# A sparse-attention and gMLP kernel: fewer row-halved score tiles, v of a pair in one load, gMLP sums in two parts, and another order

## The chip, the cores and the metric

The kernel runs on one core of a Trainium2 chip. Time is device microseconds (us) of one execution; the kernel before took 218.75 us, the median of three runs (218.19 to 218.76). The engines of the core are TensorE (PE: matmuls; PEld: its weight loads), VectorE (DVE), ScalarE (ACT), GpSimd (POOL) and SyncE (SP, which here only issues DMA). Each runs its own instructions in order and waits for others by semaphores. Matmuls write PSUM; this kernel has four banks `PSG` for general use and two double banks `PSC` for scores.

## The reference, cut

Two stages follow each other. First attention over chosen chunks of keys, for 4 batches of 8 heads, 768 positions, 64 numbers a head; then a gMLP block on the result, with 512 model and 1024 hidden columns.

```python
def _attn_ref(q, k, v):                                   # (4, 8, 768, 64) each
    k_min, k_max = ...                                    # of each chunk of 32 keys
    ub = np.sum(np.maximum(q[..., None, :] * k_min, q[..., None, :] * k_max), axis=-1)
    ub = np.where(causal, ub, -1e9)
    top_chunks = np.argsort(ub, axis=-1)[..., -6:]        # six chunks for each query
    scores = scale * np.matmul(q, k.transpose(0, 1, 3, 2))
    scores = np.where(sel & (pos[:, None] >= pos[None, :]), scores, -1e9)
    attn = softmax(scores)                                # written out in the original
    return np.matmul(attn, v)

def _moe_ref(x, w_in, g_ln, w_sg, b_sg, w_out):           # x: (4, 768, 512)
    h = gelu_tanh(x @ w_in)                               # written out in the original
    u, v = h[..., :512], h[..., 512:]
    v_n = layer_norm(v) * g_ln
    v_s = np.einsum('ts,bsd->btd', w_sg, v_n) + b_sg[None, :, None]
    return x + (u * v_s) @ w_out
```

## The kernel before

The program is a list of named operations, each with an engine, what it reads and writes, and the PSUM tile that it takes. A long string `ORDER` names all of them in the order in which they are to be issued; each engine takes those of its own from it, one after another. A word such as `ka5.1@dve` puts an operation on another engine than its usual one, and `kt1.1:0` gives it PSUM slot 0. Semaphore waits follow from the reads and writes. `FILL` puts matmuls on zeros ahead of some operations of TensorE, where it waits.

The names: for a pair p of heads (16 pairs, four to a batch) `lk lq lv` load k, q and v, `kt qt` transpose k and q on TensorE, `kn kx` take the minimum and maximum of each chunk, `ke ka kb` and `qe` take the transposed k and q out of PSUM, `qr` is the positive part of q, `qc qa qb` copy q to bf16, `ub` to `uq` select the chunks of one group of pairs, `d` copies masks into place, `vc` casts v. For a head h, `s` are its scores, `e` the exponentials, `af` the causal cut on the diagonal blocks, `pv pd` the product with v, `xr xs` the division, `xt xe` the transpose for the gMLP. For a batch, `hv gv bs ba re rp rm rn vh` make the normalised half of the hidden columns, `hu gu` the other half, `pt vs gm` the mixing over positions with `w_sg` and the product of the halves, `ou oa os` the output. `wsg wt we` load and transpose `w_sg`.

Scores have two forms. The pairs below `NHALF` are row-halved: both heads of the pair lie in one tile of 128 rows, 64 each, and their matmuls use half of the array's rows each; the mask of the chosen chunks is added by matmuls of its own, with 32 rows of contraction (lines of the kernel 719 and 726):

```python
                def sc(e, t=t, m=m, segs=segs):
                    ...
                    for (o, n, kb, q0) in segs:
                        ...
                                e.matmul(t.ap()[:, 512 * i + o + a - q0:512 * i + o + n],
                                         IND[32 * cg:32 * cg + 32, 128 * kb:128 * kb + 128],
                                         dt_[32 * cg:32 * cg + 32, a - d0:z - d0], start=fresh[i], stop=False,
                                         skip_group_check=True, tile_position=(32 * cg, 0))
                    for (o, n, kb, q0) in segs:
                        for i in range(2):
                            r = e.matmul(t.ap()[:, 512 * i + o:512 * i + o + n],
                                         KP[p][64 * i:64 * i + 64, 128 * kb:128 * kb + 128],
                                         QP[p][64 * i:64 * i + 64, q0:q0 + n], start=fresh[i], stop=True,
                                         skip_group_check=True, tile_position=(64 * i, 0))
```

All other pairs are whole: each head has a tile of its own in which k (or q) and the mask lie on different rows, so one matmul of 96 or 128 rows makes the masked score (line 766). The masks have to be copied into those rows, by small DMAs `d`:

```python
            kt_, qt_, rows = (KA[w], QA[w], slice(0, 96)) if i == 0 else (KB[w], QB[w], slice(0, 128))
            ...
                def sc(e, t=t, mms=mms):
                    for (o, n, kb, q0) in mms:
                        r = e.matmul(t.ap()[:, o:o + n], kt_[rows, 128 * kb:128 * kb + 128],
                                     qt_[rows, q0:q0 + n], start=True, stop=True, skip_group_check=True)
```

A whole pair has its k taken out of PSUM in four instructions (`ka`, `kb`), a row-halved pair in two (`ke`); its q is copied to bf16 in two instructions (`qa`, `qb`) instead of one (`qc`).

The parts of the gMLP that the change touches, each an accumulation in one PSUM bank:

```python
                def hv(e, t=t, qt=qt):
                    for dk in range(NDK):                      # 4
                        r = e.matmul(t.ap()[:, 0:F], xT[s][:, dk, 128 * qt:128 * qt + 128], winb[:, dk, F:DFF],
                                     start=(dk == 0), stop=(dk == NDK - 1))
                ...
                    def pt(e, t=t, fb=fb, tg=tg):
                        for sb in range(NT):                   # 6
                            r = e.matmul(t.ap()[:, 0:TG], vhat[s][:, sb, 128 * fb:128 * fb + 128],
                                         wsgT[:, sb, TG * tg:TG * tg + TG], start=(sb == 0), stop=(sb == NT - 1))
                ...
                    def ou(e, t=t, qt=qt):
                        for fb in range(NF):                   # 4
                            r = e.matmul(t.ap()[:, 0:DM], gT[s][:, fb, 128 * qt:128 * qt + 128], woutb[:, fb, :],
                                         start=(fb == 0), stop=(fb == NF - 1))
```

`oa` adds x to the output tile on VectorE into one of three buffers `osb`, and `os` stores it. Loads are limited to six in flight (`WINDOW`); k, q and v have three buffers each (`NQS`), in pieces of 256 bytes:

```python
            for i in range(2):
                o, pat, off = dst[s][:, :, i, :], [[DH, 128], [128 * DH, NT], [1, DH]], (2 * p + i) * S * DH
                P.op(f"l{nm[0]}{p}.{i}", "sp", lambda e, o=o, pat=pat, off=off: e.dma_start(
                    o, bass.AP(src.tensor, off, pat)),
                    writes=[(nm, s, i)], dma=f"{nm}{s}_{i}", bulk=True, cost=(560, 905), prio=prio + i)
```

Of the kernel before, what the change touches and what calls it, by code (L numbers as in the profile page):

```python
# [9 lines left out]
BF16 = mybir.dt.bfloat16  # L10
# [8 lines left out]
nh lk1.0 zB2 warm0 lk1.1 J0 lk0.0 zA0 idF lk0.1 J vx13 W02 W03 W01 W00 vx10 lq0.1 lq0.0 kt1.1:0 kt1.0:1 kn1.1 lq1.0  # L19
kn1.0 kx1.1 lq2.1 kt0.1:2 kx1.0 kt0.0:3 kn0.1 lq1.1 ke1.0 kw1@pool zA1 kn0.0 ke1.1 lq2.0 qt0.1:1 kx0.0 qt0.0:0 qe0.1  # L20
Jn kx0.1 lk2.1 qe0.0 qr0.1 kw0@pool qr0.0@act qc0 lk2.0 ke0.0 vx11 IND ub0:10 ke0.1 iB1 lq3.1 qt1.1:3 ut0.1 qt1.0:2
ut0.0 qe1.1 lq3.0 uc0.10 uc0.00 qe1.0 uc0.11 uc0.01 uc0.12 uc0.02 um0.1 qr1.0@act qc1 lk3.0 qt2.1:0 qr1.1@act um0.0
qt2.0:1 qe2.1 ud0.1 ub1:23 lk4.1 qe2.0 ud0.0 uq0.1 iA0 qr2@act uq0.0 lk3.1 kt2.1:0 ut1.0 s0.4:0 ut1.1 s0.2:1 uc1.00
e0.4 kn2.1 lk4.0 uc1.01 uc1.10 s0.3:0 e0.2 uc1.02 kx2.1 lv0.0 uc1.11 kt2.0:1 um1.0 qt3.1:2 e0.3 lv0.1 uc1.12 kn2.0
s0.0:1 ud1.0 ke2.1 lq4.1 um1.1 af1.1 s0.5:0 e0.0 idB kx2.0 lk5.0 kt3.0:3 ud1.1 e0.5 kt3.1:0 ke2.0@dve af0.0 s0.6:1
lq4.0 uq1.1 kn3.1 kt4.1:1 qe3.1 s0.1:0 e0.6 uq1.0 lk5.1 vc0 kx3.1 qt3.0:2 e0.1 s1.0:1 kn4.1 af1.0 qe3.0 lq5.0 kn3.0
ke3.1 af0.2 s1.1:0 e1.0 af1.2 kx4.1 lq6.0 pv1:2 af0.1 kx3.0 pd1 qc2 pv0:0 ka4.1 lq6.1 xr1 ke3.0@dve pd0 s1.5:1 kb4.1
af2.0 xr0 xs1 lk6.1 e1.1 qt4.0:3 kw3@pool af3.0 xs0 qt4.1:1 e1.5 kt4.0:2 lq5.1 qr3 xt0.0:0 kn4.0 kw2@pool s1.3:0 qe4.0
af2.2 lv1.1 xe0.0 qe4.1 iB3 kt5.0:3 e1.3 kx4.0 lv1.0 ub2:10 kn5.0 kw4@pool qc3 ka4.0 lk6.0 kx5.0 kb4.0 s1.2:1 ut2.0
af3.2 ka5.0 lq7.1 ut2.1 qt6.0:2 e1.2 uc2.10 uc2.00 um2.1 lv3.1 qt5.0:1 s1.6:0 kb5.0 um2.0 s1.4:1 lk7.0 vc1 qe5.0  # L30
qt5.1:0 e1.4 qt6.1:3 e1.6 ud2.1 lq7.0 kt5.1:1 ud2.0 qe5.1 uq2.1 af3.1 qe6.0 lv2.1 pv3:0 qr4@act uq2.0 af2.1 pv2:2
kn5.1 qa4 qe6.1 lv2.0 s2.0:1 qr5@act kx5.1 iA1 pd3 lv3.0 e2.0 ka5.1@dve pd2 kt6.1:3 s2.3:0 xr2 xr3 kw5@pool lk7.1
kb5.1 xs3 wsg0 s2.5:1 e2.3 kn6.1 qa5 ub4:10 xs2 e2.5 kx6.1 win0 s2.2:0 ut4.0 ka6.1 wsg5 s2.4:1 ut4.1 e2.2 zB1 uc4.00
um4.0 kt6.0:2 e2.4 s2.1:0 win2 qr6 qt7.0:1 e2.1 ud4.0 s3.4:1 kn6.0 vc2 kt7.0:0 kb6.1 uq4.0 s3.3:0 af5.0 qe7.0@dve e3.4
d4.00 qt7.1:3 kx6.0 d4.01 vc3 xt0.1:1 e3.3 qe7.1@dve s3.5:1 d5.00 ka6.0@dve wsg2 wt0:3 d5.01 e3.5 xe0.1 s3.1:0 wsg3
kb6.0 vx12 kn7.0 win1 kt7.1:1 e3.1 we0 s3.0:1 win3 kn7.1 pv5:2 e3.0 af4.0 kx7.0 pd5 pv4:3 xr5 xs5 s3.2:0 ka7.0 gln pd4
e3.2 kb7.0@dve s8h.2:1 lq9.1 wt5:2 qr7@act kx7.1 af7.0 lq10.0 s8h.1:0 we5 e8h.2 pv7:0 lv5.0 kw7@pool ka7.1@dve af6.0
e8h.1 pd7 lq9.0 pv6:2 uc4.10 xr4 xr7 s10h.0:1 xs4 kw6@pool kb7.1 qb5 pd6 s10h.1:0 xs7@act xr6 ub6:31 xs6 qb7 e10h.1
um4.1 xt0.2:0 zA2 ut6.0 e10h.0 xt0.3:2 zB0 xe0.2 s8h.0:0 wt3:3 uc6.00 xe0.3 e8h.0 iA2 wt2:0 we3 s10h.2:1 hv0.1:2 ut6.1
e10h.2 af8.0 we2 lv4.0 hv0.0:3 ud4.1 wsg1 lq8.1 hu0.30:1 uq4.1 qb4 gv0.0 d5.11 hv0.2:0 gv0.1 af10.0 bs0.0 d5.10  # L40
hv0.3:3 gu0.30 d4.11 bs0.1 gv0.2 iA3 lv4.1 hv0.4:2 ba0.0 gv0.3 bs0.2 lq8.0 hv0.5:1 gv0.4 ba0.2 d4.10 ba0.1 re0.0 bs0.3
rp0.0 lk8.0 qt9.0:0 gv0.5 qt9.1:3 rm0.0 ba0.3 hu0.01:2 bs0.4 qe9.0 lv5.1 rn0.0 qe9.1 zA3 hu0.00:1 bs0.5 vh0.0 iB0
ba0.4 hu0.31:0 ba0.5 gu0.00 lk8.1 re0.1 rm0.1 um6.0 vh0.2 rp0.1 hu0.10:3 bsg gu0.31 hu0.20:1 gu0.10 ud6.0 gu0.01 rn0.1
hu0.11:0 uq6.0 vc4 vh0.4 qt8.1:3 d7.00 gu0.20 hu0.21:2 vh0.3@dve wsg4 lk9.1 gu0.11 pv8:1 uc6.10 vh0.1 vh0.5@dve d6.01
wt1:0 gu0.21 vc5 lv6.0 s11h.0:0 we1 pd8 d6.00 s9h.0:1 qa6 xr8 pt0.01:2 xs8 lv7.1 um6.1 e9h.0 lk9.0 wo3 pv10:0 vs0.01
pd10 qe8.1 kt8.1:1 af9.0 xr10 e11h.0 s9h.1:1 kn8.1 pt0.00:2 lv6.1 iB2 xs10 e9h.1 d7.01 kx8.1 s11h.1:0 qa7 lq12.1
vs0.00 kt8.0:3 ka8.1 wt4:0 kn8.0 e11h.1 zB3 s9h.2:1 lk10.0 pt0.03:2 we4 wo0 e9h.2 kx8.0 s11h.2:0 wo2 ud6.1 kb8.1
pt0.02:0 uq6.1 gm0.01 ka8.0 d7.10 s12h.1:1 kb8.0 vs0.02 wo1 qt8.0:1 d6.11 e11h.2 pt0.10:3 gm0.00@dve d6.10 e12h.1
gm0.02 vs0.03 d7.11 s12h.2:0 pv9:0 vs0.10 e12h.2 lk11.1 gm0.03 pd9 s14h.2:1 qe8.0 xr9 kt9.0:2 xs9@act kt9.1:3 kw8@pool
kn9.0 af11.0 s12h.0:0 e14h.2 pt0.11:1 kx9.0 xt1.0 qb6 e12h.0 pt0.12:0 vs0.11 lk10.1 vc6 ka9.0 kn9.1 s14h.0:1 lv7.0  # L50
kb9.0 vs0.12 ou0.1:1 qb8 lk12.0 qr9@act lq10.1 e14h.0 s13h.0:0 gm0.10 oa0.1 pt0.13:2 kx9.1 e13h.0 af14.0 s14h.1:1
lq11.1 ou0.2:0 ka9.1 kw9 vs0.13 af12.0 e14h.1 lq12.0 s13h.1:0 oa0.2 gm0.11 kt10.1:1 os0.1 kb9.1 pv11:2 kn10.1 os0.2
e13h.1 s15h.1:1 vc7 kx10.1 pd11 lk11.0 pv12:0 xr11 e15h.1 af13.0 ka10.1@dve lq11.0 pd12 s13h.2:0 ou0.0:3 xr12 xs11
gm0.12 e13h.2 xt1.1 s15h.0:1 kb10.1 gm0.13@dve pv14:2 qr8@act pd14 s15h.2:0 xs12 qa9 lv8.1 e15h.0 pv13:1 oa0.0 pd13
qa8 ou0.5:0 e15h.2 xr14 xr13 os0.0 xs14 xs13@act ou0.4:3 af15.0 oa0.5 pv15:2 xt1.2 oa0.4 pd15 qt10.0:1 xr15 kt11.1:0
xs15 qe10.0 qt11.0:3 kn11.1 xt1.3 qe11.0 qt11.1:1 kt10.0:2 kx11.1 qe11.1 qt10.1:3 kn10.0 ka11.1 lq13.1 ou0.3:1
qe10.1@dve kb11.1 lv10.1 kx10.0 qb10 ub8:30 lv8.0 oa0.3 ka10.0 lv9.1 qb9 kb10.0 qt12.1:1 ut8.1 kt11.0:2 qe12.1 ut8.0
qa10 lv10.0 hv1.0:0 uc8.10 kn11.0 kw10@pool um8.1 hv1.1:1 gv1.0 kx11.0 hv1.2:3 ud8.1 ka11.0 bs1.0 vc8 gv1.1 hv1.5:0
uq8.1 gv1.2 uc8.00 ba1.0 hu1.30:1 d8.11 bs1.1 gv1.5 lk12.1 hv1.3:3 bs1.2 kb11.0 d9.10 qr11@act um8.0 hu1.10:0 d9.11
gv1.3 ba1.1 hv1.4:2 ba1.2 ud8.0 d8.10 gu1.30 rm1.0 gu1.10 re1.0 bs1.3 lk13.1 hu1.11:3 rp1.0 gv1.4 lk14.1 uq8.0  # L60
hu1.00:1 gu1.11 ba1.3 kw11@pool bs1.4 d9.00 rn1.0 vc10 hu1.31:0 vh1.0 d8.01 bs1.5 gu1.00 hu1.20:2 d8.00 ba1.4 vh1.1
ba1.5 qr10 hu1.21:3 gu1.20 d9.01 re1.1 vh1.2@dve gu1.31 hu1.01:1 lv11.1 gu1.21 rm1.1 rp1.1 qt12.0:2 os0.5 gu1.01
kt12.1:0 qe12.0@dve lv9.0 kt12.0:3 rn1.1 s19h.2:1 vh1.3@dve lk13.0 ub10:12 lk15.1 vh1.4@dve e19h.2 lq15.0 s18h.0:0
ut10.1 vh1.5 os0.4 s16h.0:1 ut10.0 e18h.0 kn12.1 pt1.00:2 lk14.0 uc10.00 um10.0 e16h.0 s16h.1:0 vc9 lq13.0 pt1.01:1
vs1.00 e16h.1 ud10.0 s18h.2:1 qr12 pt1.02:2 e18h.2 uq10.0 uc10.10 vs1.01 d10.00 s17h.2:0 s17h.1:1 kn12.0 d10.01 e17h.2
gm1.01 pt1.10:1 vs1.02 lv12.0 e17h.1 kx12.0 lv11.0 gm1.02 s16h.2:0 kx12.1 pt1.13:2 os0.3 e16h.2 vs1.10 af16.0 d11.00
# [32 lines left out]
"""  # L99


FILL = {"kt1.1": 7, "kt0.1": 4, "qt0.1": 1, "qt2.1": 3, "ou3.4": 1, }


class PsumTile:
# [244 lines left out]
def c_act64(n):  # L350
    t = 62 + n / 1.2 + 118
    return (t, t - 15)
# [15 lines left out]
def _kernel(nc, q, k, v, w_in, g_ln, w_sg, b_sg, w_out, out):  # L368
# [12 lines left out]
    NDK = DM // 128  # L381
    NF = F // 128
    TG = S // 2
    LEAD = 45.0
    NSOLO = 2
    NHALF = 4

# [706 lines left out]
```

The softmax here doesn't subtract the row's maximum and nothing guards it: scores larger than these inputs give would overflow.

## Time and profile before

| | |
|---|---|
| time, median of three | 218.75 us |
| profiled execution, span | 216.3 us |
| granted TensorE clock | 0.999 |
| TensorE / VectorE / ScalarE / GpSimd busy | 94% / 82% / 79% / 55% |
| DMA moved | 31.78 MB in 92542 packets, 85984 of them under 512 bytes |
| SyncE queue, share of 16 DMA engines | 61.2% |

The profile is of one execution. Its page gives busy times by engine and by group of instructions, the chain of work that ended last (followed back from the last instruction to what released it), and the DMA. The trace answers further questions: the timeline of an engine, the busy times in chosen stretches, who waited for whom. In a group or timeline row, `L766 PE MATMUL PSC<-QA,KA 96*128 96x128 bf16 x7` reads: line 766 of the kernel, TensorE, matmul, into tile `PSC` from `QA` and `KA`, a weight of 96 by 128, a moving operand of 96 rows by 128 columns, seven of them. The timeline merges neighbours of one kind, and gives the form of the first. A bracket at the end of a row holds the idle time ahead of it and what ended it.

### The profile page before, as it was taken

The numbers are of one execution on the slowest core, as the hardware profiler recorded it, in microseconds if no ns is written. First come the engines' busy times: TensorE is split into PE (matmuls) and PEld (weight loads), VectorE is DVE, ScalarE is ACT, GpSimd is POOL, SyncE is SP. The second block draws the span as 40 slices with busy tenths as digits, with TensorE's granted clock in tenths as the row PEclk, the third lists the DMA queues.
The fourth block names the chain that finished last, engine by engine and source line by source line (L and its number), as shares of the span: only waits on it lengthen the run. The fifth ranks groups of instructions, "written<-read, shape, count | busy, mean of one in ns | idle before, by whom it ended". The sixth has DMA issues, their size and how long they took to land.

```text
span 216.3 us, 6168 instructions
## 1 busy us (share of the span) xinstructions
PE 203.2 (94%) x2362; PEld 132.3 (61%) x2362; DVE 176.9 (82%) x544; ACT 170.4 (79%) x287; POOL 118.4 (55%) x177
## 2 busy tenths in 40 slices
PE   7788997999999999999999999999999999899990
PEld 2355864567567776864566778764657786345640
DVE  1999998998899978889979999889898468484871
ACT  2569998999999999978998787999997889277000
POOL 3242838968776997824414899303747666021530
PEclk9999999999999999999999999999999999999999
DMA  7999999999689979999469852920173304303033
GB/s 151 218 220 206 210 216 230 139 160 209 132 190 194 214 125 193 256 127 227 107 176 221 200 139 46 238 38 2 31 199 78 105 16 88 134 0 145 5 145 147
DMA packets 92542, 31.78 MB, mean 147 GB/s; under 512 B 85984, under 2 KB 88800, under 8 KB 92512
## 3 DMA queue, kind: packets, MB, share of 16 engines
q1 hardware_dynamic: 90496, 28.62, 61.2%
q0 software_dynamic: 2016, 2.75, 8.5%
q8 instruction: 19, 0.31, 0.6%
q14 instruction: 11, 0.09, 0.2%
HBM read 24.77 MB, written 6.29 MB: 144 GB/s over the span
## 4 chain that ended last, share of the span: by engine, by line
PE 63%; DVE 14%; DMA 10%; ACT 5%; SPq 4%; issue 2%; POOL 1%; DVEq 0%
PE PSG L920 11%; PE PSC L766 10%; PE PSG L853 9%; PE PSG L900 7%; PE PSG L512 6%; DMA out_dram<-osb 5%; PE PSG L943 5%; PE PSG L787 5%; SPq L503 3%; PE PSG L614 3%; DVE W L530 2%; DMA vn<-in_v_dram 2%; DVE osb L950 2%; DMA qn<-in_q_dram 2%; PE PSC L726 2%; PE PSG L795 2%
## 5 line engine op out<-in xcount | busy, mean ns | idle before, releaser
L770 ACT ACTIVATE E<-PSC 128x1024 bf16<-128x1024 f32 (+1 forms) x72 | 62.3, 919 | 8.1 <-PE PSC L766 7.7
L672 POOL TENSOR_SCALAR_AFFINE_SELECT E<-E 128x768 bf16<-128x768 bf16 (+3 forms) x40 | 29.1, 738 | 19.4 <-ACT E L770 11.1
L530 DVE TENSOR_REDUCE W<-PSG 128x12 f32<-128x384 f32 x64 | 34.0, 545 | 4.5 <-PE PSG L512 4.0
L920 PE MATMUL PSG<-wsgT,vhat 128*128 128x384 bf16 x192 | 35.2, 326 | 0.4 <-DVE vsT L927 0.2
L933 POOL TENSOR_TENSOR uT<-vsT,uT 128x384 bf16<-128x384 f32 x24 | 22.6, 950 | 13.5 <-DVE vsT L927 13.1
L927 DVE SCALAR_TENSOR_TENSOR vsT<-PSG,glnT,bsgbc 128x384 f32<-128x384 f32 x32 | 19.6, 612 | 9.8 <-PE PSG L920 9.6
L920 PEld LDWEIGHTS PSG<-wsgT,vhat 128*128 128x128 bf16 x192 | 17.9, 98 | 11.2 <-DVE vsT L927 0.5
L736 ACT ACTIVATE E<-PSC 128x1024 bf16<-128x1024 f32 (+3 forms) x26 | 21.7, 864 | 3.1 <-PE PSC L726 2.8
L943 PE MATMUL PSG<-woutb,uT 128*128 128x512 bf16 x96 | 23.8, 379 | 0.0
L853 PE MATMUL PSG<-winb,xT 128*128 128x512 bf16 x96 | 22.0, 379 | 0.9 <-DVE osb L950 0.9
L577 POOL CAST vx<-vn 128x768 bf16<-128x768 f32 x16 | 14.4, 899 | 15.2 <-DMA vn<-in_v_dram 15.1
L900 PE MATMUL PSG<-xT,winb 128*128 128x384 bf16 x128 | 22.6, 326 | 0.0
L950 DVE TENSOR_TENSOR osb<-PSG,XS 128x512 f32<-128x512 f32 x24 | 16.5, 688 | 6.2 <-PE PSG L943 3.7
L787 PE MATMUL PSG<-vx,E 128*128 128x65 bf16 x480 | 19.7, 193 | 1.2 <-POOL vx L577 1.2
L787 PEld LDWEIGHTS PSG<-vx,E 128*128 128x128 bf16 x480 | 17.7, 97 | 3.5 <-ACT qT L519 1.4
L766 PE MATMUL PSC<-QB,KB 128*128 128x128 bf16 (+2 forms) x168 | 19.1, 246 | 0.2 <-ACT E L770 0.2
L766 PE MATMUL PSC<-QA,KA 96*128 96x128 bf16 (+2 forms) x168 | 19.0, 246 | 0.1
L858 ACT ACTIVATE vgb<-PSG 128x512 f32<-128x512 f32 x24 | 14.0, 594 | 5.9 <-PE PSG L853 5.8
L873 POOL TENSOR_TENSOR rstd<-rstd,neghalf 128x3 f32<-128x3 f32 x8 | 7.1, 892 | 20.2 <-DVE mv L865 10.2
L900 PEld LDWEIGHTS PSG<-xT,winb 128*128 128x128 bf16 x128 | 12.4, 98 | 9.2 <-ACT uT L906 0.4
L863 DVE BATCH_NORM_STATS2 stats<-vgb 128x6 f32<-128x512 f32 x24 | 15.8, 680 | 1.8 <-ACT vgb L858 1.5
L853 PEld LDWEIGHTS PSG<-winb,xT 128*128 128x128 bf16 x96 | 9.1, 98 | 12.0 <-DVE osb L950 1.2
(85 smaller groups left out, 399.0 us busy)
## 6 DMA issues: line engine op xcount, KB each, us to landing
kn<-in_k_dram SPq DMA_DIRECT2D x32, 192.0 KB, 4.0
qn<-in_q_dram SPq DMA_DIRECT2D x32, 192.0 KB, 4.3
vn<-in_v_dram SPq DMA_DIRECT2D x32, 192.0 KB, 3.8
out_dram<-osb SPq DMA_DIRECT2D x24, 256.0 KB, 2.6
winb<-in_moe_w_in_dram POOLq DMA_DIRECT2D x4, 256.0 KB, 6.0
vhat<-in_moe_w_sg_dram POOLq DMA_DIRECT2D x3, 192.0 KB, 4.3
xT<-in_moe_w_sg_dram POOLq DMA_DIRECT2D x3, 192.0 KB, 5.3
woutb<-in_moe_w_out_dram POOLq DMA_DIRECT2D x4, 128.0 KB, 4.0
```

Of the source, the lines that this page charges most:

```text
L530: P.op(f"k{'nx'[m]}{p}.{hf}", "dve", lambda d, t=t, m=m, op=op, cs=cs: d.tensor_reduce(W[w][:, m, cs.start // 32:cs.stop // 32], t.ap()[:, ...
L672: P.op(f"af{h}.{r}", "pool", lambda g, ev=ev, cnt=cnt: g.affine_select(ev, ev, pattern=[[0, cnt], [1, 128]], compare_op=ALU.is_ge, fill=0. ...
L736: P.op(f"e{p}.{c}", "act", lambda e, t=t, o0=o0, nn=nn: e.activation(E[:, slot:slot + 2, o0:o0 + nn], t.ap().rearrange("p (i x) -> p i x", ...
L766: r = e.matmul(t.ap()[:, o:o + n], kt_[rows, 128 * kb:128 * kb + 128], qt_[rows, q0:q0 + n], start=True, stop=True, skip_group_check=True)
L770: P.op(f"e{h}h.{c}", "act", lambda e, t=t, c0=c0, c1=c1: e.activation(E[:, es, c0:c1], t.ap()[:, 0:c1 - c0], ACTF.Exp, scale=SCALE), write ...
L787: r = e.matmul(t.ap()[:, 65 * qb:65 * qb + 65], E[:, es, a:a + 128], vx[w][:, kb, i, :], start=first, stop=False, skip_group_check=True)
L853: r = e.matmul(t.ap()[:, 0:F], xT[s][:, dk, 128 * qt:128 * qt + 128], winb[:, dk, F:DFF], start=(dk == 0), stop=(dk == NDK - 1))
L900: r = e.matmul(t.ap()[:, 0:TG], winb[:, dk, 128 * fb:128 * fb + 128], xT[s][:, dk, TG * tg:TG * tg + TG], start=(dk == 0), stop=(dk == NDK ...
L920: r = e.matmul(t.ap()[:, 0:TG], vhat[s][:, sb, 128 * fb:128 * fb + 128], wsgT[:, sb, TG * tg:TG * tg + TG], start=(sb == 0), stop=(sb == N ...
L933: return d.tensor_tensor(gT[s][:, fb, TG * tg:TG * tg + TG], vsT[vs][:], uT[s][:, fb, TG * tg:TG * tg + TG], op=ALU.mult)
L943: r = e.matmul(t.ap()[:, 0:DM], gT[s][:, fb, 128 * qt:128 * qt + 128], woutb[:, fb, :], start=(fb == 0), stop=(fb == NF - 1))
L950: P.op(f"oa{b}.{qt}", "dve", lambda d, t=t, qt=qt, os_=os_: d.tensor_tensor(osb[os_][:].rearrange("p (a x) -> p a x", x=128), t.ap()[:, 0: ...
```

## The change

- `NHALF` goes from 4 to 2: pairs 2 and 3 get the whole form, so that only pairs 0 and 1 are row-halved. Buffers of the selection that were sized for the row-halved groups of two pairs become smaller (`UF`, `m8`, `Dn`, `Dt`), `rT` has two buffers instead of three.
- v of both heads of a pair is loaded by one DMA of 384 KB instead of two of 192 KB; `vn` has the two heads one after the other, and the cast reorders them.
- `hv`, `pt` and `ou` are each two operations: `hv` with three matmuls and `hw` with one, `pt` and `pu` with three each, `ou` and `ov` with two each. Other operations can stand between the two, and each waits only for its own inputs.
- Three of the six transposes of `w_sg` (`wt3`, `wt4`, `wt5`) go from TensorE to DMA (`WPE`).
- The zeros for the fillers shrink from 512 to 128 columns and are read repeatedly; the fillers stand elsewhere. A variant with k copied by DMA is there, but `KDMA = 16` leaves it unused.
- The order is new throughout.

It is meant to take work from TensorE and to let the order fill its waits.

```diff
-nh lk1.0 zB2 warm0 lk1.1 J0 lk0.0 zA0 idF lk0.1 J vx13 W02 W03 W01 W00 vx10 lq0.1 lq0.0 kt1.1:0 kt1.0:1 kn1.1 lq1.0
 ... (the order)
+J0 lk1.0 warm0 zA3 W03 W01 lk1.1 zB2 lk0.0 zB0 lk0.1 zA1 idF lq0.0 J lq0.1 kt1.1:0 kt1.0:1 kn1.1 lq1.1 W00 kn1.0 vx12
 ... (of the order after, the first scores of pairs 2 and 3 and the end)
+qt6.1:1 um2.1 e1.1 d2.01 af2.0 s1.6:1 qe5.0 vc1 d2.00 kn5.1 s1.4:0 qe6.1 qt5.1:2 ka5.0@dve e1.4 lv2 af3.2 e1.6 lq7.1
+ud2.1 qe5.1 af3.0 uq2.1 pv2:1 kb5.0 kx5.1 qa5 pd2 d2.11 qr5@act pv3:2 xr2 pd3 d2.10 xs2 ka5.1 kt6.1:0 zB3 xr3 lk7.1
+qr4@act xs3 kt6.0:1 kw5@pool qa3 lk8.1 s4h.0:0 kb5.1 kn6.1 s4h.1:1 d3.00 kn6.0 e4h.0 qb4 ub4:23 d3.01 kx6.0 e4h.1
 ...
+xs30 pd31 ov2.4 xr31 ov2.5 xs31@act oa2.4 hv3.2:0 oa2.5 xt3.3:1 hv3.0:2 xe3.3 os2.5 hv3.1:3 os2.4 hw3.2 hw3.0 gv3.2
 ...
+gm3.10@dve pu3.11 gm3.03@dve pt3.12:1 pu3.12 vs3.13 ou3.1:0 vs3.11 gm3.13 ov3.1 vs3.12 ou3.0:3 ov3.0 gm3.11 oa3.1
+ou3.2:2 oa3.0 ov3.2 os3.1 gm3.12 ou3.4:1 oa3.2 os3.0 ou3.3:0 ou3.5:3 os3.2 ov3.4 ov3.3 oa3.4 ov3.5 oa3.3 os3.4 oa3.5
+os3.3 os3.5
@@
-FILL = {"kt1.1": 7, "kt0.1": 4, "qt0.1": 1, "qt2.1": 3, "ou3.4": 1, }
+FILL = {"kt1.1": 7, "kt0.0": 4, "qt2.0": 3, "kt2.1": 1, "kt3.1": 1, "pv2": 2, }
@@
-    NHALF = 4
+    NHALF = 2
-    WPE = range(NT)
+    WPE = (0, 1, 2)
@@
-        vn = [T(f"vn{i}", [128, NT, 2, DH], F32) for i in range(NQS)]
+        vn = [T(f"vn{i}", [128, 2, NT, DH], F32) for i in range(NQS)]
-        NR = 3
+        NR = 2
@@ (in load)
+            if nm == "vn":
+                P.op(f"lv{p}", "sp", lambda e: e.dma_start(
+                    dst[s][:], bass.AP(src.tensor, 2 * p * S * DH, [[DH, 128], [128 * DH, 2 * NT], [1, DH]])),
+                    writes=[(nm, s, 0), (nm, s, 1)], dma=f"{nm}{s}", bulk=True, cost=(560, 1780), prio=prio)
+                return
@@ (in vside)
-            P.op(f"vc{p}", "pool", lambda g: g.tensor_copy(vx[w][:, :, :, 0:DH], vn[s][:]),
+            P.op(f"vc{p}", "pool", lambda g: g.tensor_copy(
+                vx[w][:, :, :, 0:DH], vn[s][:].rearrange("p i j d -> p j i d")),
@@ (hv; pt and ou likewise)
-                def hv(e, t=t, qt=qt):
-                    for dk in range(NDK):
+                for nm, dks in (("hv", range(NDK - 1)), ("hw", (NDK - 1,))):
+                    def hv(e, t=t, qt=qt, dks=dks):
+                        for dk in dks:
 ...
+                    for nm, sbs in (("pt", range(3)), ("pu", range(3, NT))):
 ...
+                    for nm, fbs in (("ou", range(2)), ("ov", range(2, NF))):
```

## The prediction

> **What bounds the kernel now.** I read the busy shares of the page first, then the chain that ended last.
>
> ```profile
> PE 203.2 (94%) x2362; PEld 132.3 (61%) x2362; DVE 176.9 (82%) x544; ACT 170.4 (79%) x287; POOL 118.4 (55%) x177
> ...
> PE 63%; DVE 14%; DMA 10%; ACT 5%; SPq 4%; issue 2%; POOL 1%; DVEq 0%
> ```
>
> TensorE is busy for 94% of the span and makes up 63% of the chain. A busy TensorE need not be streaming at its peak, so a second look is needed: the busy time by stage (columns: TensorE, weight load, VectorE, ScalarE, GpSimd, granted clock, DMA share, GB/s), with my cuts at the starts of the phases.
>
> ```profile
> 0.00:20.00 20.00, 15.91 (x190) 9.36 (x190) 14.61 (x70) 11.14 (x21) 6.73 (x19) 1.00 1.14 197
> 20.00:36.00 16.00, 14.36 (x264) 10.21 (x263) 14.73 (x52) 14.57 (x28) 10.46 (x21) 1.00 1.08 217
> 36.00:60.00 24.00, 23.90 (x369) 14.97 (x367) 21.39 (x66) 23.36 (x38) 19.17 (x30) 1.00 0.94 163
> 60.00:90.00 30.00, 30.00 (x327) 21.72 (x325) 26.76 (x73) 29.13 (x52) 24.56 (x34) 1.00 0.97 198
> ...
> 182.00:217.00 35.00, 28.23 (x171) 14.50 (x169) 20.80 (x43) 11.40 (x21) 7.11 (x9) 0.99 0.28 97
> ```
>
> From 36 to 182 us TensorE has hardly an idle microsecond. Before 36 us the loads (DMA share above 1) and the selection on VectorE set the pace; after 182 us only the last gMLP batch is left. Between 36 and 90 us ScalarE is nearly as full as TensorE: 23.36 of 24 and 29.13 of 30. So the time falls only if (a) TensorE is given less to stream, or (b) one of its remaining holes closes. To judge (a) I need the real cost of a score tile, from the timeline of TensorE. A row's duration includes the drain of the last matmul, so I take the distance from one row's start to the next row's start.
>
> ```profile
> 40.22 0.31 PE L719 MATMUL PSC<-Dt,IND 32*128 32x128 bf16 x6
> 40.47 0.40 PE L726 MATMUL PSC<-uT 64*128 64x128 bf16 x8
> 40.79 0.55 PE L512 MATMUL PSG<-identF,qn 128*128 128x128 f32 x3
> 41.27 0.39 PE L719 MATMUL PSC<-Dt,IND 32*128 32x256 bf16 x4
> 41.59 0.39 PE L726 MATMUL PSC<-uT 64*128 64x256 bf16 x4
> 41.92 0.55 PE L512 MATMUL PSG<-identF,kn 128*128 128x128 f32 x3
> ...
> 49.09 0.60 PE L766 MATMUL PSC<-QA,KA 96*128 96x384 bf16 x4
> 49.53 0.62 PE L787 MATMUL PSG<-vx,E 128*128 128x65 bf16 x15
> ```
>
> A row-halved tile of 1024 scores takes 41.27 to 41.92 = 0.65 us; a whole-array tile of 1024 scores takes 49.09 to 49.53 = 0.44 us. The halves of the two heads do run side by side, but the mask is a second pass of matmuls over nearly the same columns, which the whole-array form gets for nothing in its longer contraction (96 or 128 rows).
>
> For (b), three holes of TensorE in that timeline:
>
> ```profile
> 10.14 0.56 PE L614 MATMUL PSG<-qT,W 64*32 64x192 f32 x16 [1.00 <-ACT rT L558]
> ...
> 33.88 1.07 PE L787 MATMUL PSG<-vx,E 128*128 128x65 bf16 x30 [1.24 <-POOL vx L577]
> ...
> 187.83 2.55 PE L853 MATMUL PSG<-winb,xT 128*128 128x512 bf16 x11 [0.85 <-DVE osb L950]
> ```
>
> The second is the late v of pair 1 (its load is issued around 26 us and lands past 32 us). The third is an output buffer that waits for its store.
>
> **What the Trainium skill says.** "TensorEngine Tiling (Array Packing)", Key Properties: tiles operate independently, but changing the tiling mode drains TensorE. The trace agrees with both. In the profile three k transposes take 0.33 us when another full-array group follows (26.09 to 26.42) and 0.48 us when a row-halved tile follows (40.79 to 41.27): about 0.1 to 0.15 us is lost at each switch. "Perfetto Trace Analysis", Identifying the Most-Contended Engine, warns that matmul busy share overstates how full TensorE is; here too, since a lone group of four 512-column matmuls shows 1.03 us and occupies 0.86 (179.13 to 180.00), which is why I use start to start. The same page, Optimizing DMA Performance (What "DMA-bound" means), names two DMA limits, the engines and the issuing sequencer; the load merge touches only the second, since the pieces keep their 256 bytes.
>
> **The change part by part.**
>
> 1. *Pairs 2 and 3 whole instead of row-halved.* From the timeline, the six tiles of pair 2 start at 34.88, 36.34, 36.99, 38.66, 39.10 and 40.22 and take 0.63 + 0.65 + 0.54 + 0.44 + 0.64 + 0.57 = 3.47 us; those of pair 3 sum to 3.46 us in the same way. Sum 6.93. A whole head takes 0.44 + 0.45 + 0.28 (rows of the chain and timeline, tiles of 1024, 1024 and 640), 1.17 us; four heads 4.7 us. Saved 2.2 us. To this come the mode switches: some ten separate visits to the row-halved mode, at 0.1 us, 1.0 us. **TensorE -3.2 us**, all of it between 34 and 49 us, where TensorE is full.
>  ScalarE's exponentials stay alike (both forms cover 5376 columns in six instructions). The k evacuations grow from 4 to 8 instructions (481 to 561 ns each), the bf16 q copies on GpSimd from two of 823 ns to four of 822 to 854 ns, and eight small mask transfers are new (2.1 to 2.6 us to landing, median), which come into the way of the first scores of pairs 2 and 3.
> 2. *Three of six transposes of w_sg by DMA.* On TensorE each is six matmuls of 56 ns, 0.33 us (54.70 to 55.03): **-1.0 us**. VectorE loses three copies of 542 ns. The transfers are of the kind that takes 2.8 us for xT; w_sg is needed only when the second half of the token mixing begins, so they should be hidden.
> 3. *v of a pair in one load.* 16 fewer issues of about 0.55 us on SyncE, which mostly waits anyway. The bytes and their pieces stay. Near zero by itself; it could bring the v of pair 1 forward by one issue, but it is asked for at about the same place of the order, so I count nothing.
> 4. *hv, pt and ou in two parts.* Same matmuls, same columns: zero work. What it can give is freedom: three of four matmuls of hv can run before the last xT is there. I give it the hole at 187 us (0.85) and a few small ones: -1.0 us. At the very end it may cost: the three last second parts finish 0.43 us apart, while VectorE needs 0.69 us for each output add, so the adds queue: +0.4 us.
> 5. *Fillers* 18 instead of 16, of 215 ns each; they stand in places of waiting: +0.2 us at most.
> 6. *Engines that only get moved work*, counted in the two orders with the page's mean durations. ScalarE: four k evacuations more (+1.92), two of pair form fewer (-0.98), one q fewer (-0.50), one relu more (+0.69), three vhat fewer (3 x 0.812 = -2.44): -1.3 us. VectorE: +2.24 -1.08 +0.54 -0.65 +2.35 -0.61 -1.63 = +1.2, less 0.3 for two MAX8 of 163 ns: +0.9 us. GpSimd: 2 x (0.854 + 0.822 - 0.823) + 0.95 = +2.7 us. None of them becomes the fullest engine by this.
>
> Sum on the path: -3.2 -1.0 -1.0 +0.4 +0.2 = -4.6 us. I allow +0.3 for new waits of pairs 2 and 3, and a little more to come out of a reordering made for this: **213.8 us**, 4.95 under 218.75.
>
> **Rivals.**
>
> *A. ScalarE takes over between 36 and 90 us.* It idles only 0.64 + 0.87 = 1.5 us of these 54. If TensorE gets 4 us faster there and ScalarE doesn't, that stretch shrinks by about 1.5 us plus what the order moves out of it. For: the figures above. Against: ScalarE is idle 24 us after 182 us and 4.9 us between 100 and 140, and much of TensorE's gMLP work needs no ScalarE, so the order can shift it. This would make 216 to 217 us.
>
> *B. New waits for the mask transfers.* DMA is saturated until 40 us (share 1.08), so a mask may land 4 to 5 us after its issue, as the loads do (3.8 to 4.3 us); and GpSimd must make four bf16 copies of q where it made two. For: at 33.88 TensorE already waits for GpSimd. Against: the new order sets the masks of pairs 2 and 3 35 to 45 entries before their first use. This would cost 1 to 3 us: 215 to 217 us.
>
> *C. The reordering is worth more than I see:* stalls before 36 us (some 8 us in all, counted from start distances above each form's median) shrink too. 210 to 212 us. Against: the start is set by loads, which stay as they were.
>
> *D. The new order is simply worse on the chip*, with holes scattered over the batches. Nothing in the profile speaks for it; it would be above 219 us.
>
> **Range and chances.** I give the sum about half of the weight, A and B together a third, C an eighth, D a twentieth. The 2% line is at 0.98 x 218.75 = 214.4 us, only 0.6 us above my number, so faster by over 2% is little more than an even bet: 0.56; within 2% 0.39; slower 0.05. Eight in ten: 210.5 to 217.8 us.
>
> **What will show it.** Right, if the matmuls of lines like L719 and L726 come only in tiles of pairs 0 and 1, TensorE's busy time falls by 4 to 5 us, and no new hole over 1 us stands between 36 and 182 us. Step 1 is wrong if a score tile of pairs 2 and 3 waits for the masks or the q copies, or if ScalarE's idle time from 36 to 90 us goes to zero while TensorE gets holes. Step 2 is wrong if a token-mixing matmul waits for a w_sg transpose by DMA. Step 4 is wrong if the hole near the beginning of the last batch is still there, or the last output add ends more than 1 us later after the last matmul than before. The prediction as a whole fails if the order makes new stalls on in-order queues, which only the new trace can show.

## The result and the profile after

The changed kernel takes 220.93 us, the median of four runs (220.53 to 221.6), against 218.47 us of the kernel before in the same set: a ratio of 1.0121 (95% interval 1.0082 to 1.0161). It is slower, where I had forecast 213.8 us. In the profiled executions the span grew from 216.3 to 219.4 us.

The page of the kernel after, its busy times and its chain:

```profile
PE 200.7 (91%) x2270; PEld 133.8 (61%) x2286; DVE 173.8 (79%) x543; ACT 170.1 (78%) x286; POOL 120.2 (55%) x180
...
PE 71%; DVE 13%; DMA 5%; ACT 5%; issue 3%; SPq 1%; DVEq 0%
```

TensorE is busy for less time, in a longer span: it got idle time that it didn't have. The timeline of TensorE shows where (start, duration, then the operation; in brackets the idle time ahead of a row and what ended it).

```profile
38.86 0.45 PE L789 MATMUL PSC<-QA,KA 96*128 96x256 bf16 x3
39.89 0.60 PE L789 MATMUL PSC<-QB,KB 128*128 128x128 bf16 x7 [0.59 <-DMA QB<-Dt]
...
42.06 0.50 PE L526 MATMUL PSG<-identF,qn 128*128 128x128 f32 x3
43.74 0.60 PE L789 MATMUL PSC<-QA,KA 96*128 96x128 bf16 x7 [1.19 <-POOL E L695]
...
45.28 0.50 PE L1007 MATMUL PSG<-identB,vhat 128*128 128x128 bf16 x6
47.91 0.60 PE L789 MATMUL PSC<-QB,KB 128*128 128x128 bf16 x7 [2.13 <-DMA QB<-Dt]
...
129.23 0.35 PE L818 MATMUL PSG<-vx,E 128*128 128x65 bf16 x6
131.66 0.60 PE L789 MATMUL PSC<-QB,KB 128*128 128x128 bf16 x7 [2.07 <-issue]
```

Four first score tiles of heads wait: three of pairs 2 and 3, and one of pair 11. Two brackets name a mask transfer (`QB<-Dt`), one names GpSimd, one nothing. The landings in the trace settle all four: masks landed at 39.80, 43.65, 47.82 and 131.57 us, and each tile started 0.09 us after one of them. By distance from start to start, less what the matmul ahead takes by itself, the four holes are 0.74, 1.35, 2.29 and 2.24 us, 6.6 us in sum. After the fourth one, TensorE is slow as well, as the busy times by stretch show (last three columns: granted clock, DMA share, GB/s):

```profile
128.00:132.00 4.00, 1.93 (x52) 1.82 (x49) 2.63 (x6) 1.61 (x2) 1.47 (x2) 1.00 0.41 93
132.00:136.00 4.00, 4.00 (x21) 2.55 (x19) 2.12 (x5) 1.91 (x2) 2.72 (x4) 0.59 1.13 288
136.00:140.00 4.00, 3.94 (x53) 3.19 (x52) 2.76 (x6) 3.41 (x6) 2.00 (x3) 0.98 0.21 79
```

The 0.59 is a mean over four us: the clock records of the trace have 0.50 from 132.76 to 136.17 us, 3.41 us. Either way about 1.6 us are lost (4 x 0.41).

The two kinds of late mask are not late for the same reason. The masks of pairs 2 and 3 were issued among large loads. Ahead of the mask of pair 11, from 123 us on, only other masks and one output store had been issued. It was issued at 128.13 us; of the 16 shares in which it completes, 15 were in by 129.89 us and the last came at 131.57. At 129.19 to 130.37 us one of the 16 DMA engines moved a 16 KB piece of the queue that the page lists as `instruction` (the program's own instructions), and the last two of the mask's 32 pieces went directly behind it, at 130.34 and 130.41. So 1.7 of the 2.24 us fit a mask share that stood behind an instruction fetch. In the 16 traces of this case, masks beside which under 40 KB of other data moved took 1.21 us at the median from the end of their issue to landing when no fetch overlapped them (281 masks), and 2.19 when one did (50). No run moves a fetch, so this is a reading of the traces and not shown by experiment.

**The balance.** I split the time of TensorE in both profiles: the distance from each matmul to the next counts as work up to what its form takes at its median (216 ns for 512 columns, 162 for 384, 56 for 128, 29 for 65, 109 for an f32 transpose), and the rest counts as holes; row-tiled matmuls, which run side by side, count as work except where they stand still for longer than 0.3 us. Matmuls whose records a trace lacks (16 of 512 columns after) are put back as work.

| us | before | after |
|---|---|---|
| row-halved tiles | 14.5 | 7.7 |
| whole tiles | 27.8 | 32.5 |
| transposes by `identB` | 3.7 | 2.7 |
| fillers | 3.5 | 3.95 |
| all work | 193.4 | 190.6 |
| holes | 16.1 | 22.2 |

Work fell by 2.8 us, holes rose by 6.1, together the 3.1 us of the spans (to rounding and the tail). The holes themselves: 6.6 for the masks and 1.6 for the clock came; the wait for v of pair 1 (1.24) and that for an output buffer at 187 us (0.85) went.

### The profile page after: what moved, and what is told of

It reads as the page before. It is cut to its first block, busy times and chain, and to the rows that moved or that the text cites. A ratio compares the mean times of both kernels' runs of the same rounds, so it can differ in the third digit from the quotient of the medians.

```text
span 219.4 us, 5993 instructions
## 1 busy us (share of the span) xinstructions
PE 200.7 (91%) x2270; PEld 133.8 (61%) x2286; DVE 173.8 (79%) x543; ACT 170.1 (78%) x286; POOL 120.2 (55%) x180
## 4 chain that ended last, share of the span: by engine, by line
PE 71%; DVE 13%; DMA 5%; ACT 5%; issue 3%; SPq 1%; DVEq 0%
PE PSC L789 14%; PE PSG L945 13%; PE PSG L876 8%; PE PSG L924 8%; PE PSG L970 8%; PE PSG L526 7%; PE PSG L810 6%; DVE W L544 5%; DMA QB<-Dt 4%; PE PSG L637 3%; PE PSG L818 2%; ACT XS L833 2%; DVE m L661 2%; DMA kn<-in_k_dram 1%; ACT uT L930 1%
## 5 line engine op out<-in xcount | busy, mean ns | idle before, releaser
L793 ACT ACTIVATE E<-PSC 128x1024 bf16<-128x1024 f32 (+1 forms) x84 | 73.9, 917 | 13.6 <-PE PSC L789 12.4
L695 POOL TENSOR_SCALAR_AFFINE_SELECT E<-E 128x768 bf16<-128x768 bf16 (+3 forms) x40 | 29.6, 748 | 23.7 <-ACT E L793 20.7
L945 PE MATMUL PSG<-wsgT,vhat 128*128 128x384 bf16 x192 | 37.8, 331 | 0.0
L789 PE MATMUL PSC<-QB,KB 128*128 128x128 bf16 (+2 forms) x196 | 23.5, 250 | 5.0 <-DMA QB<-Dt 2.7
L789 PE MATMUL PSC<-QA,KA 96*128 96x128 bf16 (+2 forms) x196 | 22.5, 246 | 1.2 <-POOL E L695 1.2
L970 PE MATMUL PSG<-woutb,uT 128*128 128x512 bf16 x83 | 22.2, 379 | 0.7
L789 PEld LDWEIGHTS PSC<-QB,KB 128*128 128x128 bf16 x196 | 14.9, 99 | 10.9 <-issue 5.0
L789 PEld LDWEIGHTS PSC<-QA,KA 96*128 96x128 bf16 x196 | 14.3, 97 | 7.6 <-ACT E L793 2.6
L526 PE MATMUL PSG<-identF,kn 128*128 128x128 f32 x96 | 16.3, 291 | 0.8 <-DMA kn<-in_k_dram 0.5
L526 PE MATMUL PSG<-identF,qn 128*128 128x128 f32 x96 | 15.1, 279 | 1.5 <-DVE U L656 0.6
```

The lines of the kernel that those rows point to most:

```text
L526: r = e.matmul(t.ap()[:, 128 * j:128 * j + 128], src[:, 3 * hf + j].rearrange("p i d -> p (i d)"), identF[:], is_transpose=True)
L695: P.op(f"af{h}.{r}", "pool", lambda g, ev=ev, cnt=cnt: g.affine_select(ev, ev, pattern=[[0, cnt], [1, 128]], compare_op=ALU.is_ge, fill=0. ...
L793: P.op(f"e{h}h.{c}", "act", lambda e, t=t, c0=c0, c1=c1: e.activation(E[:, es, c0:c1], t.ap()[:, 0:c1 - c0], ACTF.Exp, scale=SCALE), write ...
```

## The experiments

Ratios are to the kernel before, measured together with the version named, with their 95% intervals. "Masks" are the transfers `d`.

**Masks of pairs 2 and 3 earlier.**

```diff
 (order) zB3 behind iA3; d3.00 d3.01 behind d2.00; d2.11 d2.10 d3.10 d3.11 behind uq2.1
```

> The changed kernel with the mask transfers of pairs 2 and 3 issued ahead of three loads, in one go (and the zeros of QB 3 set earlier, which the masks need). Theory M (late masks): TensorE stood still 0.74 + 1.35 + 2.29 = 4.4 us between 39 and 48 us, each time until a mask landed; most of it goes: 216.5 to 218 us, 3 to 4 us under the changed kernel. Theory O (the order is too tight anyhow: ScalarE or GpSimd would have stopped TensorE a moment later): 220 to 221 us, with new holes between 39 and 50 us.

1.0202 (1.0132 to 1.0273): no gain. The masks of the second head of pair 2 were issued at 38.4 and 39.2 us and landed at 43.0 and 43.2 us, 4.0 to 4.6 us later, behind v of pair 2 (384 KB) and q of pair 7 (192 KB) in the same queue; TensorE stood still for 2.93 us there. About 1.3 us of that is one share again: 15 of the 16 of the first of these masks were in by 41.70 us, the last at 42.98, with an instruction fetch between. This kernel also keeps the hole of pair 11 (2.65 us here), so it isn't a clean test of pairs 2 and 3; "both shifts" below is. Both theories missed the point: it isn't the issue alone that is late.

**Masks of pair 11 earlier.**

```diff
-d10.01 ... d10.00 d11.11 ... d10.10 d11.01 d11.00 d10.11 d11.10
+d10.01 ... d10.00 d11.11 d11.10 ... d10.10 d11.01 d11.00 d10.11
```

> The changed kernel with the two masks of the second head of pair 11 issued third and fourth of their eight instead of third and last. Theory M: the hole of 2.24 us at 129.4 us goes, and with it the stretch from 132 to 136 us in which the granted clock was lower (some 1.4 us): 217.0 to 218.5 us. If the lower clock has nothing to do with the hole: 218.5 to 219. Theory O: within 0.5 us of 220.9.

1.002 (0.9997 to 1.0043), 1.0 point under the 1.0121 of the changed kernel. The mask landed 1.79 us after its issue, the hole of 2.24 us and the slow stretch are gone (granted clock of 124 to 138 us: 1.00 instead of 0.88). The mask that is now last in the row takes 3.51 us, with a fetch beside it once more, but its tile comes later and doesn't wait. So one badly placed mask costs 1%. This kernel is the base of what follows.

**Both shifts.**

> Both shifts of mask transfers together, nothing else. Theory M: the gains add: 213 to 215 us, clearly faster than the kernel before. Theory O: above 218 us, because other waits take the place of these.

1.0075 (1.0049 to 1.01). Pair 11 is mended, but pairs 2 and 3 have one hole of 3.05 us at 39.4 us instead of three smaller ones, and the granted clock of 36 to 50 us is 0.88. Here too 15 of 16 shares of the mask were in by 40.97 us and the last at 42.24, past a fetch.

**Pairs 2 and 3 row-halved again, in the new order.**

```diff
-    NHALF = 2
+    NHALF = 4
 (order) s4h, s5h, e4h, e5h -> s2.0 to s2.5, e2.0 to e2.5; likewise pair 3; ka, kb -> ke; qa, qb -> qc; no d2, d3
```

> The changed kernel and its order, but pairs 2 and 3 row-halved again: no mask transfers for them, their score tiles in the same places. Theory M: the 4.4 us of holes between 39 and 48 us go, and 3.2 us of TensorE work come back: 219 to 220.5 us, the hole at 129 us stays. Theory O: the work comes back on top of the holes: 223 to 225 us.

1.0055 (1.0019 to 1.009). The holes between 39 and 48 us are gone, and so is that at 130 us (its mask landed at 130.72 us and its tile started 0.09 us later, so it is still on the edge). By the split of time its work is 192.9 us, 2.5 more than with the whole form on the masks11 base (190.5), and its holes are 17.4 against 18.6. So in net the whole form gains about what the two ratios say, 0.3%, which the intervals don't separate from nothing.

This run says something more. It is the change without its first part: no new mask waits, no hole at 130 us, and still it is slower than the kernel before, where the prediction had the other parts at -1.4 us. Part of it are waits for ScalarE: 1.0 us for an exponential at 50.5 us, and brackets of 0.89, 0.26 and 0.27 us for `uT` between 68 and 71 us. So the late masks aren't the whole loss.

**The loads behind the masks.**

```diff
 (order) as in masks_both, and lv2 ahead of d2.01; d2.11 d2.10 d3.10 d3.11, then lv3 lq7.1, behind uq2.1
```

> Both shifts of masks, and besides the loads of that stretch (v of pair 3, q and k of pair 7) are issued behind all eight masks of pairs 2 and 3, v of pair 2 ahead of them. Theory Q (a mask waits in the DMA queues behind the bytes issued just before it: 576 KB at some 210 GB/s are 2.7 us on top of the 1.8 us that a mask takes alone): all eight land within 2.6 us of their issue, the holes between 39 and 48 us shrink from some 3.5 us to under 1.2 us, and the time falls to 0.98 to 0.99 of the kernel before. Theory S (the small transfers are slow in themselves or while anything else runs): landing stays at 3.5 to 4.7 us, and the ratio at 1.00 to 1.01.

1.0187 (1.013 to 1.0243). Queue theory Q is right on the landing: all eight masks landed 1.8 to 2.5 us after issue, and no score tile waited for one. But the time didn't fall. The timeline of TensorE in this kernel:

```profile
41.07 0.62 PE L788 MATMUL PSC<-QB,KB 128*128 128x128 bf16 x7 [0.36 <-ACT E L792]
41.52 0.50 PE L855 MATMUL PSG<-identB,XS 128*128 128x128 bf16 x6
46.13 0.87 PE L525 MATMUL PSG<-identF,qn 128*128 128x128 f32 x3 [4.11 <-issue]
```

Now the transpose of q of pair 7, whose load had been held back, stands 4.1 us and stops every matmul behind it: the load was issued at 39.81 us and landed at 46.04, 0.09 us before the row.

**Only what isn't urgent held back.**

```diff
 (order) d2.11 d2.10 lv2 lq7.1 behind uq2.1; d3.* behind lk7.1; lk8.1 lq8.0 lq8.1 behind d5.01
```

> The kernel with the masks of pair 11 moved up (1.002), and in the stretch of pairs 2 and 3 only so much moved as is not urgent: the masks of the second heads of pair 2 ahead of v of pair 2 and q of pair 7, those of pair 3 right behind k of pair 7, and the loads of pair 8 (576 KB, needed some 15 us later) behind all masks up to pair 5. Theory Q: the masks of pair 2 land about 2 us after issue, those of pair 3 within 4 us; the k of pair 7 is there in time; of the 3.6 us of holes between 39 and 48 us at most 1.5 stay: ratio 0.988 to 0.995. Theory T (the DMA queues are the limit of this stretch, and every reshuffle only moves the wait to another transfer): 1.00 to 1.01, with a hole in front of another transfer.

1.021 (1.0118 to 1.0302). Theory T. The masks of the second head of pair 2 landed in 1.7 and 1.8 us, and TensorE waited elsewhere:

```profile
43.17 0.72 PE L525 MATMUL PSG<-identF,qn 128*128 128x128 f32 x3 [2.30 <-DVE KA L534]
...
55.91 0.52 PE L525 MATMUL PSG<-identF,qn 128*128 128x128 f32 x3 [2.19 <-DMA qn<-in_q_dram]
```

The second is q of pair 8, which I had taken for not urgent: the new order wants it at 53.6 us. The first is q of pair 7 again, though its bracket names VectorE: that load was issued at 37.30 us and landed at 43.08, 0.09 us before the row. Some 1.4 us of this wait are one late share past a fetch (15 of 16 in by 41.64), so crowded queues explain it in part.

**No wait for the masks of pairs 2 and 3.**

```diff
+                        if p < 4:
+                            dst = SCR[64 * (p % 2) + 32 * i:64 * (p % 2) + 32 * i + 32, q0:q0 + nq]
-g.memset(QA[i][64:96, 0:LO], 0.0)
+g.memset(QA[i][64:96, 0:(S if i >= 2 else LO)], 0.0)
```

The masks of these four heads are moved as before, into a tile that nobody reads; the heads take zeros, so their selection of chunks is left out.

> The kernel with the masks of pair 11 moved up (1.002), but the masks of pairs 2 and 3 go into a scratch tile: the same transfers at the same times, but the scores of those four heads take zeros in place of their masks and wait for none of them (so their selection of chunks is left out). The zeros cost GpSimd some 1 us more at the start. Theory M: the holes between 39 and 48 us (3.6 us) go and nothing comes in their place: ratio 0.983 to 0.989, about where the prediction put the whole change (0.979). Theory T: ScalarE, GpSimd or a load stops TensorE in the same stretch: 0.995 to 1.003.

0.9956 (0.9916 to 0.9995), 0.6 points under its base (0.9997 to 1.0043): the intervals are barely apart. An execution more than 1.5% above the fastest of its kernel stays out of the ratios; here that leaves out four of ten, and the median of all ten, 217.35 us, is level with the 217.28 us of the kernel before. By the ratio only some 1.4 us of the 3.6 us of waits came off the time. The busy times of 36 to 48 us suggest why; first the base (masks11):

```profile
36.00:48.00 12.00, 8.65 (x123) 6.36 (x121) 9.89 (x29) 9.43 (x14) 11.35 (x19) 1.00 1.03 188
```

and without the wait:

```profile
36.00:48.00 12.00, 11.10 (x167) 8.37 (x166) 11.69 (x35) 11.92 (x18) 11.23 (x19) 1.00 0.93 183
...
60.00:72.00 12.00, 10.84 (x94) 6.94 (x92) 9.45 (x42) 10.12 (x20) 6.93 (x11) 1.00 0.74 131
```

The first four pairs of numbers are TensorE, weight load, VectorE and ScalarE. ScalarE goes from 9.43 to 11.92 of 12 us: it looks like the next limit, and TensorE still doesn't fill (11.10, where the kernel before had 12.00). Part of the gain is given back between 60 and 72 us, where TensorE is busy for 10.84 of 12 (12.00 in the base):

```profile
65.61 0.82 PE L926 MATMUL PSG<-xT,winb 128*128 128x384 bf16 x4 [0.48 <-ACT uT L932]
66.69 0.62 PE L812 MATMUL PSG<-vx,E 128*128 128x65 bf16 x15 [0.26 <-ACT uT L932]
67.77 0.82 PE L926 MATMUL PSG<-xT,winb 128*128 128x384 bf16 x4 [0.27 <-ACT uT L932]
```

Those rows wait for ScalarE to empty PSUM through the gelu, as they do in the row-halved version above (0.89, 0.26 and 0.27 us) and don't in the base. No run lightens ScalarE, so that it is the limit is argued and not shown.

**The split of the sums undone.**

```diff
 (order, on the masks11 base) each hv, pt, ou moved down to stand directly ahead of its hw, pu, ov
```

> The kernel with the masks of pair 11 moved up (ratio 1.002 to the kernel before), and each first part of hv, pt and ou moved down directly ahead of its second part, so that the split is undone while the rest of the order stands. If the freedom is worth 1 us as predicted: ratio 1.006 to 1.010. If it is worth nothing: 1.000 to 1.004. It is no pure undoing of an order made without the split.

1.0316 (1.0265 to 1.0367), 3% over its base, more than I had thought. Its profiled execution took 227.2 us, 2.3 above the median. There the holes for the masks are 2.04 and 2.70 us, where the base has 1.50 and 1.43 at the same tiles, the granted clock drops after them (47.2 to 50.6 us), and new holes of 0.9 to 1.1 us stand behind exponentials at 120 and 168 us. This order leans on the split; what the split would be worth in an order made without it, this doesn't say.

**All w_sg transposes on TensorE, and v in two loads.**

```diff
-    WPE = (0, 1, 2)          (m11_wtpe; wt3 wt4 wt5 with PSUM slots, we3 we4 we5 added)
+    WPE = range(NT)
-            if nm == "vn":   (m11_vtwo; each lv in the order becomes two)
```

> The same base with all six transposes of w_sg on TensorE and their copies on VectorE, as in the kernel before. If the three DMA transposes are worth the 1.0 us of TensorE work: ratio 1.006 to 1.008. If their place was free on TensorE: 1.002.

> The same base with v of a pair in two loads of 192 KB, one behind the other. Predicted worth of the merge: nothing, so 1.000 to 1.004. If the bigger load delays the masks behind it, the two loads at the window of six in flight would be better: 0.995 to 1.000; if the issues on SyncE count, worse: 1.005 to 1.010.

1.0102 (1.0042 to 1.0162) and 1.0078 (1.0049 to 1.0106), against 1.002 of the base. Taken alone, both parts look worth more than I gave them, though the first interval touches that of the base. But each also shifts the moments of all later transfers in a kernel whose masks are on edge: the first has a hole for a mask that ends at 41.1 us (bracket 1.91 us) and a lower clock from 42.5 us on, the second one of 2.25 us at 46 us. So I tried them in the old order.

**The single parts in the kernel before.**

```diff
 b_v   : v of a pair in one load, at the place of the first of the two
 b_wt  : WPE = (0, 1, 2), wt3 wt4 wt5 in their old places
 b_vwt : both
```

> The kernel before with only this part of the change: v of a pair in one load, at the place of the first of the two; all else and the order as before. By the experiment on the changed kernel the merge is worth 0.6%: ratio 0.993 to 0.996. By the prediction nothing: 0.998 to 1.002.

> The kernel before with only this part: transposes 3, 4 and 5 of w_sg by DMA, in the same places of the order. By the prediction 1.0 us less on TensorE: ratio 0.993 to 0.997. If their places were filled waits: 1.000.

> The kernel before with both of these parts. If they add: 0.987 to 0.993; if neither carries over into the old order: 1.000.

0.9971 (0.9958 to 0.9984), 1.0134 (1.0062 to 1.0207) and 1.019 (1.0123 to 1.0257). b_v helps by 0.3%, and is the only complete version whose interval lies below 1. The waits say how; before:

```profile
POOL vx L577 <- DMA vn<-in_v_dram: 15.1, 5, 5.2
...
PE PSG L787 <- POOL vx L577: 1.2, 1, 1.2
```

and with one load (us in total, times, longest):

```profile
POOL vx L581 <- DMA vn<-in_v_dram: 2.1, 2, 1.5
```

GpSimd's waits for v fall from 15.1 to 2.1 us, and TensorE's wait for that cast isn't listed any more. That doesn't show that one load is better than two. In the order of the kernel before, the two loads of a pair stand 6 to 127 entries apart, so b_v also asks for the second half earlier. With the two loads directly one behind the other (m11_vtwo), GpSimd waits 4.5 us for v, against 4.4 with one load (masks11). Those two point to the earlier request; b_v with two loads side by side wasn't run. The w_sg transposes by DMA do harm in the old order, and the timeline shows the place:

```profile
76.28 0.50 PE L511 MATMUL PSG<-identF,qn 128*128 128x128 f32 x3
79.47 0.81 PE L919 MATMUL PSG<-wsgT,vhat 128*128 128x384 bf16 x4 [2.69 <-issue]
```

`wt4` was issued at 73.96 us, wanted at 76.6 and there at 79.4: 5.4 us, where such a transfer takes 2.8 us at the median. In the trace of b_vwt it landed 5.7 us after its issue, and TensorE stood still for 4.52 us with the clock at half from 81.17 to 84.58 us.

**The same with that transpose earlier.**

```diff
 (order of b_vwt) wsg4 behind wsg1; wt4 ahead of lk9.1
```

> The kernel before with v in one load and three w_sg transposes by DMA (1.019), with the load of the fifth block of w_sg some 5 us earlier and its DMA transpose issued some 7 us earlier. If the late landing of this one transpose was the whole loss: 0.989 to 0.996, less than the 0.997 of the one load of v alone. If the DMA transposes disturb the loads of k and q in that stretch whenever they run: 1.005 to 1.02.

0.9996 (0.9968 to 1.0024). With one load and its transpose moved, the loss of 1.9% is gone: it was the late landing of that transfer. But the 1.0 us of work that leaves TensorE brings nothing on top: in the profiled execution (219.25 us, 1.4 above the median) new holes of about 1 us stand at 64.8 us and, for a mask, at 78.8 us.

## Why the prediction was wrong

**Step 1, the saved work:** right in size for the tiles (14.54 + 27.83 = 42.4 us before, 7.7 + 32.5 = 40.2 after, -2.2 as worked out). Of the 1.0 us for mode switches the trace has up to 0.8: entries into row-tiled work fell by eight (25 to 17), and the matmul ahead of one takes 0.096 us more than usual at the median; the balance counts that among the holes. TensorE's busy time fell by 2.5 us (203.2 to 200.7), not by 4 to 5. The row of 0.48 us at 40.79 that the prediction calls k transposes is one of q; a k row ahead of a switch (39.74 to 40.22) takes the same.

**Where it failed:** the term "I allow +0.3 for new waits of pairs 2 and 3". The mechanism stood there as rival B, with 4 to 5 us from issue to landing and 1 to 3 us of cost. What stands in the trace is 2.5 to 5.9 us to landing and 4.4 us of holes at these pairs; with the wait taken out, the time fell by 0.6 points. The argument that I set against it, "35 to 45 entries before their first use", counted words of an order and not microseconds: the last masks of pair 3 were issued at 42.4 us and wanted at 45.6. I had the landing times of the kernel before at hand (3.9 to 5.8 us for its masks issued at 43 to 45 us) and should have laid them against the issue. That kernel was on the edge too. Its first whole head is scored at 48.48 us:

```profile
48.48 0.44 PE L766 MATMUL PSC<-QA,KA 96*128 96x256 bf16 x3
...
50.88 0.60 PE L766 MATMUL PSC<-QA,KA 96*128 96x128 bf16 x7
```

The first of these starts 0.9 us after its mask landed (47.57), the second 0.09 us after (50.79), with a hole of some 0.25 us. The change brought the first whole heads forward to 38.86 us without more distance from their masks.

**What I had not thought of:** that the new order would put another mask, 90 us later, on edge (2.24 us and 1.6 us of clock). With the masks of pair 11 alone put right the loss is gone within the interval: 1.0 point, the largest piece that a run shows. The sum of the parts, 0.979, is still 2.3 points away from there, and the waits of pairs 2 and 3 are 0.6 of these.

**Rival A** is the likely second limit, though it didn't get to act in the changed kernel: with the wait for masks taken away, ScalarE is full between 36 and 48 us, and the ratio stops at 0.9956 instead of my 0.979. So in this order, even without late masks, the sum of work saved does not come off the time. Why the last 1.7 points stay away is argued from the busy times alone. That order was made with other waits in it, and an order made for this case might do better; it wasn't tried.

**Rival D**, holes scattered over the batches and a time above 219 us, got the number, and in part the cause: the row-halved version, without the late masks, is at 1.0055. **Rival C** found nothing: the stalls ahead of 36 us did not shrink (about 10 us in both).

**Step 2** gave the work (3.7 to 2.7 us) and misjudged "they should be hidden": in the changed kernel no token-mixing matmul waits for such a transfer, in the old order one did, for 2.7 us. **Step 3** "near zero": the single load, together with the earlier request, was worth 0.3% in the old order, and the profile after no longer has the 1.24 us wait for v of pair 1; for the merge by itself nothing is shown against near zero. **Step 4** held at the beginning of the last batch: the hole of 0.85 us at 187 us is gone. The +0.4 us at the very end didn't come: 5.5 us from the start of the last matmul to the end, in both. **Step 5** cost 0.45 us of work. **Step 6**, ScalarE by -1.3 us, came out at -0.3 (170.4 to 170.1), VectorE by +0.9 at -3.1 (176.9 to 173.8), GpSimd by +2.7 at +1.8 (118.4 to 120.2). Taken together, steps 2 to 5 were to bring 1.4 us, and the row-halved version, which has them and not step 1, is 1.2 us slower than the kernel before.

**What stays open.** The ratios of masks23, masks_both and the two kernels with loads moved are each the outcome of a different set of waits; I read from them that moving one transfer moves the wait, and not how much a perfect order could gain. Nor has a run moved an instruction fetch, or made ScalarE lighter. On the granted clock the traces offer a pattern. In all 16 of them the clock changes only at whole multiples of 3.41 us after its first change, and what decides seems to be how much of such a window TensorE was busy:

```profile
129.35:132.76 3.41, 1.34 (x19) 0.97 (x17) 1.31 (x3) 1.48 (x2) 2.23 (x3) 1.00 0.68 171
132.76:136.17 3.41, 3.41 (x15) 2.19 (x14) 2.12 (x5) 1.59 (x2) 1.96 (x3) 0.50 1.12 281
44.01:47.42 3.41, 1.77 (x22) 1.45 (x18) 2.05 (x4) 2.05 (x2) 3.39 (x7) 1.00 0.96 170
47.42:50.83 3.41, 2.92 (x48) 2.31 (x49) 1.63 (x5) 2.28 (x4) 1.44 (x3) 1.00 1.14 210
```

A window in which TensorE was busy for 1.34 us (first row) was followed by half clock, one with 1.77 us (third row) was not: the hole of 2.29 us straddles the border of two windows. From 30 us on, all ten drops in the 16 traces follow a window of at most 1.50 us, and only one such window (1.40 us, in masks23) has no drop behind it. In the first 25 us the pattern doesn't hold (drops after 1.43 to 2.25 us, none after one of 1.72). It is seen and not tested.

## What to carry to other kernels

Work saved on the fullest engine counts only if nothing that replaces it must come by DMA in a stretch where the queues are full: here masks that landed in 1.8 to 2.5 us with the loads held behind them took up to 5.9 us among them, and in quiet stretches too one share of a transfer could come more than 1 us after the others, beside an instruction fetch. An in-order engine that meets such a transfer early stops for everything behind. Before you trust an order, lay the issue time plus the measured landing time of every small transfer against the start of its first reader, in microseconds. And when a wait is taken away, look at once at how full the next engine is in that stretch.

## What I had not expected of the hardware

- The same small mask transfer (18 KB) landed in 1.7 to 1.8 us on a quiet queue and in up to 6.0 us between 36 and 50 us, behind loads of 192 and 384 KB; with those loads held behind it, in 1.8 to 2.5 us at the same place.
- A hole of 2.24 us of TensorE was followed by 3.41 us at a granted clock of 0.50; one of 2.29 us, at 45.6 us of the same execution, was not. "TensorE: Matmul & The Clock Gate" of the Trainium skill, What's actually happening, has a clock that falls to half after an idle window of some 3.4 us which runs freely; holes shorter than that window sufficed here, and the clock of the 16 traces does change on a fixed grid of 3.41 us.
- A transfer counts as landed with its last share: 15 of 16 shares of the mask of pair 11 were in 1.76 us after its issue, the last after 3.44 us, directly behind a 16 KB instruction fetch of 1.17 us.
